# Attention's products as 64x64 tiles in one keys-values section, with its steps named one by one

## The chip, the cores and the metric

The kernel runs on one core of a Trainium2 chip. The metric is the device time of one execution in microseconds (us), the median of several runs.

## The reference

Linear attention over 8 batches, 8 heads, 576 positions and 64 columns per head, followed by a gated feed-forward block that mixes positions. In numpy, cut to what is computed:

```python
kv  = einsum('bhsd,bhse->bhde', k, v)            # keys-values, 64x64 per head
out = einsum('bhsd,bhde->bhse', q, kv)
out = out / sqrt(mean(out*out, -1) + 1e-6) * g_norm
x   = out.transpose(0, 2, 1, 3).reshape(B, S, H * D)      # 8 x 576 x 512
h   = maximum(x @ w_in, 0);  u, v = h[..., :512], h[..., 512:]
v_n = (v - mean(v)) / sqrt(var(v) + 1e-6)
v_s = einsum('ts,bsd->btd', w_spatial, v_n) + b_spatial
y   = (u * v_s) @ w_out                          # 8 x 576 x 512
```

Inputs and outputs are float32.

## The kernel before

Heads go in pairs: four pairs per batch, each 128 columns wide (two heads of 64). The 576 positions are four chunks of 128 and a tail of 64. Feed-forward products are split into a high and a low part and done as three matmuls each in the faster format; attention's own products are plain f32, and each of those shows as two matmul records in the trace.

Per batch the work on TensorE (PE) has these stages, named by the PSUM tiles that they write:
- `psh`: the v half of `x @ w_in`, 4 chunks of 12 products with 512 columns (`hv`), in every second batch also the tails of two batches (`hv_tail`);
- `psua`, `psub`, `psuc`: the u half, 14 steps of 6 products with 288 columns (`u_steps`);
- `psa`, `psb`, `psc`: the mixing over positions and the gate, 14 steps of 6 or 8 products with 288 columns (`sp_steps`, stage p);
- `pso` on `WO`: the output products, 12 with 512 columns per chunk (`out_unit`).

Between them stand the steps of attention for the next batch, its *target batch*:
- keys-values (`pskv`, `att_four`): per pair 10 products, 128 positions by 64 columns by 64 columns, the tail padded with zeros to 128 rows; the results are copied into the diagonal blocks of `KVB` by VectorE (DVE) and ScalarE (ACT);
- queries of pairs 0 and 1 (`pso` on `KVB`, `att_two`): 32 products on 64x64 tiles into two banks, one per half of the rows; then the four pairs' tail queries (`pst`), 64 by 128 columns;
- queries of pairs 2 and 3 (`att_qa`): four products each of 128x128, on a `KVB` block whose off-diagonal quarters are zero;
- a norm per pair (`two_norm`, `norm_a`, `norm_b`), a transpose (`pstr`, `att_t`; `pstt` for the tail) and a split into `XH` and `XL` (`split_x`: ACT for the high part, DVE for the low one).

All of these use three PSUM banks in one pool (`ps_att`, bufs=3); the feed-forward products use four others.

At a batch's start `x_sums` makes eight additions of `XH` and `XL` on DVE and splits four of the sums into `T` and `UX`. `UX` and `WO` share one place in SBUF: `to_u` loads `UX` after the last output product, `to_out` loads `WO` again after the last u product, both from the POOL queue. Keys and values of pairs 2 and 3 are loaded into the place of `U` (`KVU`) once the gates have read it. Loads of keys, values and queries and stores of the output share the queue of SyncE (SP), which issues in order.

What sets the order: text strings hold one token per step. `PLAN` is the opening (to about 77 us). Behind it `FIRST` (batch 1), `EVEN` and `ODD` name v, u, p and o for the next step of each stage, `k` for `att_four` of the next batch, and `s` for the next step of a queue of attention steps, which `att_steps` fills in a fixed order. `SEVEN` and `GATED` hold the order within the u stage and stage p. From this the framework's scheduler builds one static queue per engine: it takes instructions by priority and dependency, and may place an instruction earlier or later than the text has it. Products of attention that are chained (`issue_after`, `high_priority`) follow each other as one run where nothing keeps them.

Of the kernel before, what the change touches and what calls it, by code (L numbers as in the profile page):

```python
# [8 lines left out]
F32 = mybir.dt.float32  # L9
# [34 lines left out]

SEVEN = """

p10 p11 p50 p21 p61 p60 p70 p51 p71 p31 p30 p20 p41 p40
"""
GATED = """

p10 p60 p11 p50 p70 p20 p21 p40 p61 p51 p30 p71 p41 p31
"""
FIRST = """

p p p s p p p p s p s s s p p p p s p p w s o s s o o o w o s s l
# [18 lines left out]
def body(ctx: ExitStack, tc, qT, kvm, kvt, g2, w_in, wsT, bsp, w_out, out):  # L74
# [94 lines left out]
    def tail_queries():  # L169
        return QS.rearrange("q j t -> q (j t)").rearrange("q (p t) -> q p t", t=TAIL)  # L170

    def att_four(b, st):
        banks = [b == 2 and i == 0 or ps_att.tile([P, 512], F32, name="pskv", tag="att") for i in range(2)]
        first = []

        def matmul(*args, **kw):
            if not first:
                first.append(nc.tensor.matmul(*args, **kw).ins)
                return
            with tc.high_priority(), tc.issue_after(first[0]):  # L180
                first[0] = nc.tensor.matmul(*args, **kw).ins  # L181

        for i, ps in enumerate(banks):
            if b == 2 and i == 0:
                continue
            both = ps[:, 0:2 * P].rearrange("p (j e) -> p j e", e=P)
            for j in range(2):
                kv, kt, _ = keys.pop((b, 2 * i + j))
                for c in range(NC + 1):
                    of = kv[:, :, c] if c < NC else kt  # L190
                    for h in (0, D):
                        matmul(both[h:h + D, j, h:h + D], of[:, 0, h:h + D], of[:, 1, h:h + D],
                               start=c == 0, stop=c == NC)
            own = slice(2 * i, 2 * i + 2)
            nc.vector.tensor_copy(KVB[0:D, own, 0:D], both[0:D, :, 0:D])
            nc.scalar.copy(KVB[D:P, own, D:P], both[D:P, :, D:P])
        for p in range(NP):
            st[p] = KVB[:, p]
        att_two(b, st, matmul)
        st["tail"] = ps_tail.tile([P, 512], F32, name="pst", tag="tail")[:, 0:2 * P]  # L200
        for p in range(NP):
# [5 lines left out]
    def att_two(b, st, matmul):  # L207

        qts = [queries.pop((b, i)) for i in range(2)]
        st["two"] = [ps_att.tile([P, 512], F32, name="pso", tag="att") for _ in range(2)]  # L210
        for c in range(NC):
            for j in range(2):
                for half in (0, D):
                    for h in (0, D):
                        at, t = (j * NC + c) * D, c * P + half
                        matmul(st["two"][h // D][half:half + D, at:at + D], qts[j][h:h + D, t:t + D],
                               st[j][h:h + D, h:h + D], start=True, stop=True)

    def two_norm(st, h):
# [3 lines left out]
        nc.scalar.activation(x, heads(ps), AF.Square)  # L223
        nc.vector.tensor_reduce(ss, x, axis=AX.X, op=ALU.add)
        r = rsqrt(ss, 8, P, 1.0 / D, "h")
        nc.vector.tensor_tensor(x, heads(ps), r.unsqueeze(2).broadcast_to([P, 8, D]), op=ALU.mult)
        st[h] = X2[h]
# [95 lines left out]
    def att_q(b, p, st):  # L323
        att_qa(b, p, st, b > 1 and True)
        att_qb(b, p, st)

    def tail_a(b, st, accumulate=False, soon=False):
        st["xt"] = norm_a(st["tail"], P, accumulate, soon)

# [36 lines left out]
    def att_steps(b):  # L366

        st = states.setdefault(b, {})

        def t2():  # L370
            att_t(b, 2, st)
            tail_a(b, st)
            tail_b(b, st)

        def tail():
            tail_a(b, st)
            tail_b(b, st)

        K = [lambda p=p: att_k(b, (p, p + 1), st) for p in (0, 2)]
        Q = [lambda p=p: att_q(b, p, st) for p in range(NP)]  # L380
        T = [lambda p=p: att_t(b, p, st) for p in range(NP)]
        end = lambda: att_tail(b, st)
        if b > 1:
            N = [lambda h=h: two_norm(st, h) for h in range(2)]
            late = [T[0], T[1], Q[2], Q[3], T[2], T[3]]
            if b % 2 == 0:
                return [*[K[0], lambda: att_four(b, st)] * (b == 2), *N, *late[:4], t2, T[3], end], []
            return [*N, lambda: (tail_a(b, st, soon=True), tail_b(b, st)), end], [*late, move_tail]
        if b % 2 == 0:
            return [*K[:1], Q[0], Q[1], T[0], *K[1:], Q[2], T[1], Q[3], t2, T[3], end], []  # L390
        return K + [tail, end], [Q[0], Q[1], T[0], Q[2], T[1], Q[3], T[2], T[3], move_tail]


    def three(ps, pairs):

# [620 lines left out]

    ahead(len(todo))

    def first():

        for c in (0, 2, 1, 3):
            hv(1, c)
            step()
        for d in range(4):
            if d == 2:
                enqueue(2)
            for j in range(2):
                u_unit(1, d, j)
                step()
            if d < 2:  # L1030
                make_out(2 + d)
                split_out(2 + d)
                if loads:
                    loads.pop(0)()

    def batch(b):

        if b > 1:
            to_u()
            x_sums()  # L1040
        v, u, p, o = [0, 2, 1, 3], u_steps(), sp_steps(b), [0, 1] + [NC] * (b % 2) + [2, 3]
        n_w = 0
        for token in (FIRST if b == 1 else ODD if b % 2 else EVEN).split():
            if token == "v":
                hv(b, v.pop(0))
            elif token == "u":
                u.pop(0)()
                if not u:
                    to_out()
                    if b % 2 == 0:  # L1050
                        enqueue(b + 1, 1)
            elif token == "p":
                p.pop(0)()
            elif token == "k":
                if b + 1 < NB:
                    att_four(b + 1, states.setdefault(b + 1, {}))
                enqueue(b + 1)
            elif token == "l":
                if b + 2 < NB:
                    for p in (2, 3):  # L1060
                        att_load(b + 2, p, "e")
            elif token == "o":
                out_unit(b, o.pop(0))
            elif token == "s":
                step()
            elif token == "y":
                step(len(queue))
                hv_tail()
            elif token == "w":
                w_sums(n_w)  # L1070
                n_w += 1
        if b % 2 == 0:
            step(len(queue))

    first()
    for c in range(NC):
        out_unit(0, c)
        step()
    for b in range(1, NB):
        batch(b)  # L1080


_OUTS = [((B, S, DM), "float32")]
# [41 lines left out]
```

## Time and profile before

| | us |
|---|---|
| three runs | 493.8, 493.88, 494.62 |
| median | 493.88 |
| profiled execution | 492.32 |
| its span (first to last instruction) | 490.5 |
| PE busy | 479.6 (98%) |
| DVE busy | 383.0 (78%) |
| ACT busy | 276.1 (56%) |
| share of PE in the chain that ended last | 85% |

Busy time of PE counts overlapping matmuls as modelled by the profiler; what a product costs in a run of products is the distance from its start to the next start. Views used below: the page's head, the list of what each engine waited for, the timeline of one engine in a short stretch, busy times by stretch, the chain that ended last, and groups of instructions by line.

### The profile page before, as it was taken

Reading aid. Unit: us, or ns where it says so; the run is one execution under the profiler, and the core shown is the slowest. Engines: PE = TensorE matmul, PEld = TensorE weight load, DVE = VectorE, ACT = ScalarE, POOL = GpSimd, SP = SyncE. Lnnn points to the kernel's source line nnn. Section 1 sums busy time; section 2 is a strip of 40 time slices with the busy share of each in tenths; the row PEclk is TensorE's granted clock in tenths of the full one; section 3 lists DMA queues with packets and bytes.
Section 4 is the critical chain, followed back from the end, with each engine's and each line's share of the span. In section 5 each row is a group of like instructions: output and inputs, shape, how many; then the busy total and the mean of one; then the engine's idle time right before and its main releaser. Section 6 shows DMA issues by size and latency. Waiting matters only on the chain.

```text
span 490.5 us, 10188 instructions
## 1 busy us (share of the span) xinstructions
PE 479.6 (98%) x3804; PEld 432.9 (88%) x3804; DVE 383.0 (78%) x1029; ACT 276.1 (56%) x818; POOL 35.7 (7%) x71
## 2 busy tenths in 40 slices
PE   6999989999999999999999999999999999999996
PEld 6879988999988899889987899879998889989995
DVE  2889888885977797777895798977887779877770
ACT  3899745867426782378324684257633678246322
POOL 5001100000111010010000000010000101010000
PEclk9999999999999999999999999999999999999999
DMA  8999333643368036461635426362424702333403
GB/s 263 366 303 322 95 103 99 195 165 117 111 244 249 12 91 244 158 209 45 214 126 166 151 76 229 116 194 97 119 99 145 219 1 69 137 103 113 143 31 107
DMA packets 30357, 74.13 MB, mean 151 GB/s; under 512 B 6786, under 2 KB 9858, under 8 KB 28772
## 3 DMA queue, kind: packets, MB, share of 16 engines
q1 hardware_dynamic: 24628, 47.25, 29.9%
q0 software_dynamic: 5456, 25.87, 15.9%
q8 instruction: 30, 0.49, 0.4%
q10 hardware_dynamic: 224, 0.36, 0.2%
q14 instruction: 19, 0.16, 0.1%
HBM read 58.09 MB, written 13.11 MB: 145 GB/s over the span
## 4 chain that ended last, share of the span: by engine, by line
PE 85%; DVE 3%; ACT 2%; DMA 2%; issue 0%; DVEq 0%
PE pso L398 21%; PE psh L431 16%; PE psb L638 7%; PE psub L638 6%; PE psa L638 6%; PE psc L638 5%; PE psuc L638 4%; PE psua L638 4%; PE pskv L181 3%; PE psu L398 3%; PE pstr L341 2%; PE pso L313 2%; DMA stage<-w_out 2%; PE psh L398 2%; PE pso L181 1%; PE psc L644 1%
## 5 line engine op out<-in xcount | busy, mean ns | idle before, releaser
L398 PE MATMUL pso<-WO,G 128*128 128x512 f32 x384 | 95.6, 395 | 0.0
L398 PEld LDWEIGHTS pso<-WO,G 128*128 128x128 f32 x384 | 70.6, 188 | 15.1 <-issue 0.9
L434 ACT CAST G<-SUMg 128x288 fp32r<-128x288 f32 (+1 forms) x56 | 22.2, 405 | 62.0 <-DVE SUMg L660 62.0
L740 ACT COPY o<-pso 128x512 f32<-128x512 f32 x35 | 19.7, 588 | 53.1 <-PE pso L398 44.2
L435 DVE TENSOR_TENSOR VL<-v,VH 128x512 fp32r<-128x512 f32 (+1 forms) x60 | 36.4, 615 | 10.9 <-ACT VH L434 10.6
L431 PE MATMUL psh<-WVH,XH 128*128 128x512 f32 x112 | 43.8, 391 | 0.0
L431 PE MATMUL psh<-WVH,XL 128*128 128x512 f32 x112 | 43.7, 391 | 0.0
L431 PE MATMUL psh<-WVL,XH 128*128 128x512 f32 x112 | 43.6, 390 | 0.0
L434 ACT CAST VH<-v 128x512 fp32r<-128x512 f32 (+1 forms) x60 | 32.8, 563 | 11.9 <-DVE v L463 11.3
L418 ACT ACTIVATE v<-v,mv,rv 128x512 f32<-128x512 f32 x28 | 22.8, 813 | 7.7 <-DVE mv L417 6.1
L410 DVE BATCH_NORM_STATS2 s<-v 128x6 f32<-128x512 f32 x32 | 22.1, 691 | 5.4 <-ACT v L404 4.7
L638 PE MATMUL psb<-WSH,VH 128*128 128x288 f32 x84 | 25.1, 300 | 0.0
L431 PEld LDWEIGHTS psh<-WVH,XL 128*128 128x128 f32 x112 | 21.0, 188 | 4.6
L435 DVE TENSOR_TENSOR G<-SUMg,G 128x288 fp32r<-128x288 f32 (+1 forms) x56 | 23.4, 420 | 2.2
L431 PEld LDWEIGHTS psh<-WVL,XH 128*128 128x128 f32 x112 | 21.0, 188 | 4.4
L431 PEld LDWEIGHTS psh<-WVH,XH 128*128 128x128 f32 x112 | 21.0, 188 | 4.3
L638 PE MATMUL psb<-WSL,VH 128*128 128x288 f32 x84 | 24.7, 295 | 0.0
L638 PE MATMUL psb<-WSH,VL 128*128 128x288 f32 x84 | 24.1, 294 | 0.0
L404 ACT ACTIVATE v<-psh 128x512 f32<-128x512 f32 x32 | 19.1, 598 | 6.3 <-PE psh L431 5.8
L334 ACT ACTIVATE XH<-pstr,gcol 128x512 fp32r<-128x512 f32 x28 | 18.7, 688 | 5.3 <-PE pstr L341 5.3
L638 PE MATMUL psa<-WSH,VH 128*128 128x288 f32 x72 | 21.5, 298 | 0.0
L638 PE MATMUL psa<-WSH,VL 128*128 128x288 f32 x72 | 21.2, 295 | 0.0
(281 smaller groups left out, 1410.9 us busy)
## 6 DMA issues: line engine op xcount, KB each, us to landing
WO<-spare_o POOLq DMA_DIRECT2D x12, 1024.0 KB, 7.0
KV<-kvm SPq DMA_DIRECT2D x19, 512.0 KB, 6.2
UX<-spare_u POOLq DMA_DIRECT2D x18, 512.0 KB, 6.1
out<-o SPq DMA_DIRECT2D x32, 256.0 KB, 2.2
qt<-qT SPq DMA_DIRECT2D x28, 256.0 KB, 4.1
U<-kvm SPq DMA_DIRECT2D x12, 512.0 KB, 4.1
stage<-w_in SPq DMA_DIRECT2D x8, 512.0 KB, 7.4
stage<-w_out SPq DMA_DIRECT2D x4, 512.0 KB, 6.2
```

The costliest lines, as they stand in the source:

```text
L181: first[0] = nc.tensor.matmul(*args, **kw).ins
L313: nc.tensor.matmul(ps[:, c * P:(c + 1) * P], qt[:, c * P:(c + 1) * P], st[p], start=True, stop=True)
L334: nc.scalar.activation(hi, ps, AF.Copy, scale=gcol)
L398: nc.tensor.matmul(ps, lt, rh, start=i == 0, stop=i == n - 1)
L404: nc.scalar.activation(v, ps, AF.Relu)
L410: nc.vector.bn_stats(s6, v)
L418: nc.scalar.activation(v, v, AF.Identity, bias=m, scale=r)
L431: nc.tensor.matmul(ps, lt, rh, start=k == 0 and i == 0, stop=k == NP - 1 and i == 2)
L434: nc.scalar.copy(hi, x)
L435: nc.vector.tensor_tensor(lo, x, f32(hi), op=ALU.subtract)
L638: nc.tensor.matmul(ps, lt, rh, start=start and i == 0, stop=stop and i == len(pairs) - 1, skip_group_check=True)
L740: nc.scalar.copy(o, ps)
```

## The change

From target batch 2 on:
- the queries of pairs 2 and 3 are done as those of 0 and 1 (`att_two` with `first=2`): 32 products on 64x64 tiles into two banks, normed by `two_norm`, which for them takes 8 small squares per half with a running sum;
- the tail queries are 64x64 tiles on two banks (`att_q4`), normed by `two_tail`;
- from batch 3 on the keys-values of all four pairs are one section (`kv_four`) in the order 2, 3, 0, 1, on two banks. The key tails of two pairs lie in one tile of 128 rows, loaded by one DMA, and are 64-row products at the section's end. Batch 2 keeps its two halves (`att_k`, `kv_two`);
- the queue of steps is gone. Each step has its own token: k keys-values, q first queries and tail queries, L second queries, N M n m norms, 0 to 3 transposes, x and e the tail, j the moved tail columns, Q a part of w_out. All five strings are new, `START` replaces `first()`, and `run` replaces `batch`.

The diff, cut to its core:

```diff
 GATED = """
-p10 p60 p11 p50 p70 p20 p21 p40 p61 p51 p30 p71 p41 p31
+p11 p10 p60 p50 p70 p61 p20 p21 p40 p51 p30 p71 p41 p31
 EVEN = """
-k s v v u y v u v s s u u u s u u s u s u s u s u u u s u p p s p p p s p p s s p s s s p p s p p p
-p o o l o o s
+k q u v x v e v u y u v u u u u N u u M u u u u u 1 p p 0 p p p p L p p m p p n p p p 2 p o l o o 3
+j o
 ODD = """
-v v k v v s u u u u u u u u u u s u u u u p s s p p s p s p p p p s s p p p p s p s p o l o s s o o
+k v u v u v q v u M u u u u u u u u u u p N 1 0 p L n m p p p p p p p p 2 p x e 3 p p p o l o o o
 o
@@ att_load
-            (nc.scalar if (b, p) == (0, 0) else nc.sync).dma_start(kt[0:TAIL], kvt[b, p])
+            if b < 3:
+                (nc.scalar if (b, p) == (0, 0) else nc.sync).dma_start(kt[0:TAIL], kvt[b, p])
+            else:
+                kt = KT[2 + p // 2]
+                if p % 2 == 0:
+                    nc.sync.dma_start(kt, kvt[b, p:p + 2].rearrange("p t x e -> (p t) x e"))
@@
-    def att_four(b, st):
...
+    def att_q4(b, st, matmul):
         att_two(b, st, matmul)
-        st["tail"] = ps_tail.tile([P, 512], F32, name="pst", tag="tail")[:, 0:2 * P]
-        for p in range(NP):
-            r, c = slice(p % 2 * TAIL, (p % 2 + 1) * TAIL), slice(p // 2 * P, (p // 2 + 1) * P)
-            matmul(st["tail"][r, c], tail_queries()[:, p], st[p], start=True, stop=True)
+        st["tail"] = [ps_tail.tile([P, 512], F32, name="pst", tag="tail"),
+                      ps_att.tile([P, 512], F32, name="pst", tag="att")]
+        for j in range(2):
+            for i in range(2):
+                p, r, c = 2 * j + i, slice(i * TAIL, (i + 1) * TAIL), slice(j * D, (j + 1) * D)
+                for h in (0, D):
+                    matmul(st["tail"][h // D][r, c], tail_queries()[h:h + D, p],
+                           KVB[h:h + D, p, h:h + D], start=True, stop=True)
         issue()
         issue()
+    def kv_four(b, matmul):
+
+        banks = [ps_att.tile([P, 512], F32, name="pskv", tag="att") for _ in range(2)]
+        both = [ps[:, 0:2 * P].rearrange("p (j e) -> p j e", e=P) for ps in banks]
+        of = {p: keys.pop((b, p)) for p in range(NP)}
+        order = (2, 3, 0, 1)
+        for n, p in enumerate(order):
+            kv, to = of[p][0], both[p % 2]
+            for c in range(NC):
+                for h in (0, D):
+                    matmul(to[h:h + D, p // 2, h:h + D], kv[:, 0, c, h:h + D], kv[:, 1, c, h:h + D],
+                           start=n < 2 and c == 0, stop=False, skip_group_check=True)
+        for j in (1, 0):
+            kt = of[2 * j][1]
+            for i in range(2):
+                r = slice(i * TAIL, (i + 1) * TAIL)
+                for h in (0, D):
+                    matmul(both[i][h:h + D, j, h:h + D], kt[r, 0, h:h + D], kt[r, 1, h:h + D],
+                           start=False, stop=True, skip_group_check=True)
+        for i in range(2):
+            nc.vector.tensor_copy(KVB[0:D, i:NP:2, 0:D], both[i][0:D, :, 0:D])
+            nc.scalar.copy(KVB[D:P, i:NP:2, D:P], both[i][D:P, :, D:P])
@@ att_two(b, st, matmul, first=0)
-            for j in range(2):
+            for j in (1, 0):
                 for half in (0, D):
-                    for h in (0, D):
+                    for h in (D, 0):
@@ two_norm(st, h, first=0)
+        if first:
+            for k in range(8):
+                nc.scalar.activation(x[:, k], ps[:, k * D:(k + 1) * D], AF.Square,
+                                     accum_out=ss[:, k:k + 1])
@@ two_tail(st, soon)
+        for h in range(2):
+            nc.scalar.activation(own[h], ps[h], AF.Square)
+        nc.vector.tensor_reduce(ss, heads(x), axis=AX.X, op=ALU.add)
+        r = rsqrt(ss, 4, P, 1.0 / D, "h").rearrange("p (j g) -> p j g", g=2)
+        for h in range(2):
+            nc.vector.tensor_tensor(own[h], ps[h], r[:, :, h].unsqueeze(2).broadcast_to([P, 2, D]),
+                                    op=ALU.mult)
```

What that makes of the queues, at three places. In these rows a count behind x is of instructions; a row names line, operation, output and inputs, and the output's shape.

PE at the end of batch 2's output stage (target batch 4), before: two keys-values runs of one pair (`pskv`) stand between output products, the second with the queries behind it.

```order
L398 MATMUL pso_2612<-WO,G 128x512
L181 MATMUL pskv<-U 64x64 x8
L181 MATMUL pskv<-KT_106 64x64 x2
L398 MATMUL pso_2632<-WO,G 128x512 x7
L398 MATMUL pso_2648<-WO,G 128x512
L181 MATMUL pskv<-U 64x64 x8
L181 MATMUL pskv<-KT_107 64x64 x2
L181 MATMUL pso<-KVB,qt 64x64 x32
L181 MATMUL pst<-KVB,QS 64x128 x4
L398 MATMUL pso_2648<-WO,G 128x512 x6
L431 MATMUL psh<-WVH,XH 128x512
```

The other two pairs' run (10 products each, on `KV_102` and `KV_103`) stood in the middle of stage p. The same place after:

```order
L463 MATMUL pso_2681<-WO,G 128x512 x3
L187 MATMUL pskv<-U 64x64
L190 MATMUL pskv<-U 64x64 x15
L190 MATMUL pskv<-KV_102 64x64 x8
L190 MATMUL pskv<-KV_103 64x64 x8
L190 MATMUL pskv<-KT_107 64x64 x4
L190 MATMUL pskv<-KT_106 64x64 x4
L496 MATMUL psh<-WVH,XH 128x512
```

One run of 40 products stands behind all output products; the queries and tail queries have moved on into the psh stage, 24 psh and 12 psua products later.

PE in batch 2's u stage, before: the two query products of 128x128 (x4 each) stand apart.

```order
L431 MATMUL psh<-WVH,XL 128x512
L313 MATMUL pso<-KVB,qt 128x128 x4
L638 MATMUL psuc<-T,UX 128x288 x6
...
L638 MATMUL psub<-T,WUL 128x288
L313 MATMUL pso<-KVB,qt 128x128 x4
L638 MATMUL psub<-T,UX 128x288 x6
```

After, the second queries are one run there, 6 psub products behind the last psh; the 8 transposes of pairs 0 and 1 stand 42 products ahead (24 psh, 6 psuc, 6 psua and these 6 psub):

```order
L496 MATMUL psh<-WVH,XL 128x512
L703 MATMUL psub<-T,WUH 128x288 x2
L703 MATMUL psub<-T,WUL 128x288
L703 MATMUL psub<-T,WUH 128x288 x2
L703 MATMUL psub<-T,WUL 128x288
L187 MATMUL pso<-KVB,qt 64x64
L190 MATMUL pso<-KVB,qt 64x64 x31
L703 MATMUL psub<-T,UX 128x288 x6
```

The 128x128 query products are gone, and 32 products of 64x64 stand in one place.

DVE at the turn from batch 1 to batch 2, after: the copies into `KVB` stand behind the last of the eight additions of `x_sums` and ahead of the four splits into `T`.

```order
L607 TENSOR_TENSOR SUMu_111<-SUMu_111,SUMp_110 128x576
L608 TENSOR_TENSOR SUMg<-SUMg,SUMu_111 128x576
L240 COPY KVB<-pskv 64x2x64 x2
L500 TENSOR_TENSOR T<-SUMu_111,T 128x576
L500 TENSOR_TENSOR T<-SUMp_110,T 128x576
```

Before, one copy stood in stage p and one behind the additions; now both stand behind them.

## Rows read from the trace of the kernel before

**Rows 1.** The page's head: span, TensorE's busy time, its granted clock

```profile
span 490.5 us, 10188 instructions
...
PE 479.6 (98%) x3804; PEld 432.9 (88%) x3804; DVE 383.0 (78%) x1029; ACT 276.1 (56%) x818; POOL 35.7 (7%) x71
...
PEclk9999999999999999999999999999999999999999
```

**Rows 2.** What PE waited for: us in total, times, longest

```profile
PE pskv L236 <- DMA KV<-kvm: 2.9, 3, 1.5
PE pstr L341 <- DVE x L305: 1.3, 1, 1.3
PE pso L313 <- ACT KVB L254: 1.1, 2, 0.8
```

**Rows 3.** Busy by stretch: stretch, length, PE, PEld, DVE, ACT, POOL, clock, DMA

```profile
268.00:326.50 58.50, 58.48 (x481) 52.57 (x480) 47.13 (x127) 32.98 (x100) 3.78 (x7) 1.00 0.44 147
326.50:384.50 58.00, 58.00 (x480) 52.38 (x479) 46.92 (x129) 30.59 (x96) 2.67 (x5) 1.00 0.41 134
```

**Rows 4.** PE's timeline, stage p: start, length, line, tiles, shapes, count

```profile
300.06 0.27 PE L181 MATMUL pskv<-KV 128*64 128x64 f32 x1
...
301.37 0.40 PE L638 MATMUL psc<-WSH,VH 128*128 128x288 f32 x1
```

**Rows 5.** PE's timeline in the output stage that follows

```profile
319.05 0.62 PE L398 MATMUL pso<-WO,G 128*128 128x512 f32 x2
319.61 0.69 PE L181 MATMUL pskv<-U 128*64 128x64 f32 x16
...
320.34 2.11 PE L398 MATMUL pso<-WO,G 128*128 128x512 f32 x8
322.38 0.69 PE L181 MATMUL pskv<-U 128*64 128x64 f32 x16
...
323.11 1.16 PE L181 MATMUL pso<-KVB,qt 64*64 64x64 f32 x64
324.20 0.66 PE L181 MATMUL pst<-KVB,QS 128*64 128x128 f32 x8
324.79 0.51 PE L398 MATMUL pso<-WO,G 128*128 128x512 f32 x1
```

**Rows 6.** The chain that ended last: start, length, what

```profile
285.40 0.89 PE pso L313 x8
...
289.48 0.89 PE pso L313 x8
...
346.38 2.41 PE psub L638 x18
...
428.66 8.94 PE pso L398 x39
```

**Rows 7.** PE's timeline: two first output products

```profile
197.48 0.63 PE L398 MATMUL pso<-WO,G 128*128 128x512 f32 x2
...
310.64 0.39 PE L398 MATMUL pso<-WO,G 128*128 128x512 f32 x1
```

**Rows 8.** DVE's timeline: the last addition

```profile
204.73 0.76 DVE L543 TENSOR_TENSOR SUMg<-SUMg,SUMu 128x576 f32<-128x576 f32 x1
```

**Rows 9.** Groups by line: shapes, count, busy us, mean ns, idle before

```profile
L335 DVE SCALAR_TENSOR_TENSOR XL<-pstr,gcol,XH 128x512 fp32r<-128x512 f32 x28 | 20.5, 739 | 0.2 <-ACT XH L334 0.2
...
L334 ACT ACTIVATE XH<-pstr,gcol 128x512 fp32r<-128x512 f32 x28 | 18.7, 688 | 5.3 <-PE pstr L341 5.3
...
L195 DVE COPY KVB<-pskv 64x128 f32<-64x128 f32 x11 | 3.1, 280 | 8.6 <-PE pskv L181 8.5
...
L196 ACT COPY KVB<-pskv 64x128 f32<-64x128 f32 x11 | 2.9, 260 | 6.3 <-DVE KVB L195 6.2
```

**Rows 10.** POOL's timeline: the weights' reload issued

```profile
297.84 1.11 POOL L979 DMA_DIRECT2D WO<-spare_o  x2 [6.09 <-PE psuc L638]
```

**Rows 11.** Tile WO: its loads and stores, issue to landing

```profile
DMA to landing us min/median/max: 2.0/5.4/10.0
```

More of the change, by code (lines that the diff above doesn't have):

```diff
@@ L170, in tail_queries, with chain @@
         return QS.rearrange("q j t -> q (j t)").rearrange("q (p t) -> q p t", t=TAIL)
-    def att_four(b, st):
-        banks = [b == 2 and i == 0 or ps_att.tile([P, 512], F32, name="pskv", tag="att") for i in range(2)]
-        first = []
+    def chain(behind=None):
+        last = []
         def matmul(*args, **kw):
-            if not first:
-                first.append(nc.tensor.matmul(*args, **kw).ins)
+            if not last:
+                with tc.issue_after(behind) if behind else ExitStack():
+                    last.append(nc.tensor.matmul(*args, **kw).ins)
@@ L197, in att_four @@
[L197 to L203 removed]
+            with tc.high_priority(), tc.issue_after(last[0]):
+                last[0] = nc.tensor.matmul(*args, **kw).ins
@@ L204, in att_four, with kv_two @@
         issue()
         issue()
-    def att_two(b, st, matmul):
-        qts = [queries.pop((b, i)) for i in range(2)]
+    def kv_two(b, matmul):
+        ps = ps_att.tile([P, 512], F32, name="pskv", tag="att")
+        both = ps[:, 0:2 * P].rearrange("p (j e) -> p j e", e=P)
+        for j in range(2):
+            kv, kt, _ = keys.pop((b, 2 + j))
+            for c in range(NC + 1):
+                of = kv[:, :, c] if c < NC else kt
+                for h in (0, D):
+                    matmul(both[h:h + D, j, h:h + D], of[:, 0, h:h + D], of[:, 1, h:h + D],
+                           start=c == 0, stop=c == NC)
+        nc.vector.tensor_copy(KVB[0:D, 2:4, 0:D], both[0:D, :, 0:D])
+        nc.scalar.copy(KVB[D:P, 2:4, D:P], both[D:P, :, D:P])
@@ L219, in two_norm @@
-    def two_norm(st, h):
+                               KVB[h:h + D, first + j, h:h + D], start=True, stop=True)
+    def two_norm(st, h, first=0):
         ps = st["two"][h]
@@ L325, in att_q, with two_tail @@
         att_qb(b, p, st)
+    def two_tail(st, soon):
+        if soon:
+            x = work.tile([P, 512], F32, name="xt", tag="stg", bufs=2)[:, 0:2 * P]
+        else:
+            x = X2[0][:, 0:2 * P]
+        own = [x.rearrange("p (j g e) -> p j g e", g=2, e=D)[:, :, h] for h in range(2)]
+        ps = [b[:, 0:2 * D].rearrange("p (j e) -> p j e", e=D) for b in st["tail"]]
+        ss = small.tile([P, 8], F32, name="ss", tag="ss")[:, 0:4]
+        for h in range(2):
[5 more added lines that the diff above has]
+                                    op=ALU.mult)
+        st["xt"] = x
     def tail_a(b, st, accumulate=False, soon=False):
@@ L1017, in body, with run, outs, hvs @@
     ahead(len(todo))
[L1019 to L1032, printed above, removed]
+    def run(b, tokens, v, u, p, o):
+        n_w, made = 0, iter((2, 3))
+        for x in tokens.split():
+            if x in "kqLNMnm0123xej":
+                if b + 1 < NB:
+                    att_token(x, b + 1)
+                continue
+            row.clear()
+            if x in "vupo":
+                {"v": v, "u": u, "p": p, "o": o}[x].pop(0)()
+                if x == "u" and not u and b > 1:
+                    to_out()
+            elif x == "l":
+                if b + 2 < NB:
+                    for i in (2, 3):
+                        att_load(b + 2, i, "e")
+            elif x == "y":
+                hv_tail()
+            elif x == "w":
+                w_sums(n_w)
+                n_w += 1
+            elif x == "Q":
+                k = next(made)
+                make_out(k)
+                split_out(k)
                 if loads:
                     loads.pop(0)()
-    def batch(b):
+    def outs(b):
+        return [lambda c=c: out_unit(b, c) for c in [0, 1] + [NC] * (b % 2) + [2, 3]]
+    def hvs(b):
+        return [lambda c=c: hv(b, c) for c in (0, 2, 1, 3)]
+    run(1, START, hvs(1), [lambda d=d, j=j: u_unit(1, d, j) for d in range(4) for j in range(2)], [], outs(0))
+    for b in range(1, NB):
         if b > 1:
@@ L1040, in batch @@
             x_sums()
[L1041 to L1080, printed above, removed]
+        run(b, FIRST if b == 1 else ODD if b % 2 else EVEN, hvs(b) * (b > 1), u_steps() * (b > 1), sp_steps(b), outs(b))
 _OUTS = [((B, S, DM), "float32")]
```

88 lines of the change are left out of this document (45 added, 43 removed).

## The prediction

> **What bounds the kernel now.** I began with the page's head: TensorE (PE) is busy for 479.6 of 490.5 us, at the full clock in all 40 slices [rows 1]. Busy time is modelled, so I went on to the wait list of PE: its longest entries, 2.9 and 1.3 us on L236 and L341, belong to the opening, and the same list asked for from 77.5 us on is empty [rows 2]. In the middle of the kernel one batch takes about 58 us, in which PE is busy throughout and VectorE (DVE) for 47 us, ScalarE (ACT) for 31 to 33 us [rows 3]. So behind the opening the time is the sum of what stands in PE's queue. Work taken out of that queue shortens the kernel by as much, as long as nothing makes PE wait; work moved on other engines is worth nothing by itself.
>
> So the prediction has two halves: how much shorter PE's queue becomes, and whether the new order makes it wait.
>
> **PE's queue, before.** In the timeline I read starts, not durations, because neighbouring matmuls overlap; the gap from one start to the next is what an instruction costs. An f32 product is two records (the program has 32 query products where the trace has x64). For a target batch from 3 on, attention's products stand in five places:
> - keys-values of two pairs in stage p, 40 records: 300.06 to 301.37, 1.31 us [rows 4];
> - one pair between output products, 20 records: 319.61 to 320.34, 0.73 us [rows 5];
> - the other pair, then the queries of two pairs as 64x64 tiles, then the tail queries: 322.38 to 324.79, of which 0.73, 1.09 (64 records) and 0.59 us [rows 5];
> - two query products of 128x128 (pairs 2 and 3), 0.89 us each [rows 6].
>
> Going from 128x128 work to narrow tiles and back costs too: the eight output products between the two sections take 2.04 us [rows 5] where 39 of them back to back take 8.94, or 0.229 each [rows 6], so eight should take 1.83. One leaving and one entering cost 0.21 us; three sections, 0.63. Sum before: 1.31 + 0.73 + 2.41 + 1.78 + 0.63 = **6.86 us per batch**.
>
> **PE's queue, after.** Rates from the same rows: 20 more keys-values records cost 1.31 - 0.73 = 0.58 us, 0.029 each, and what is left of 0.73, 0.15, is the fixed part of a run in one form. A 64x64 record then costs (1.09 - 0.15) / 64 = 0.0147. The new order has, per batch,
> - one section with 32 keys-values products and 8 of the tails as 64x64 tiles: 64 x 0.029 + 0.15 = 2.01, and 16 x 0.0147 + 0.15 = 0.39;
> - the first queries and the tail queries in one form: 80 x 0.0147 + 0.15 = 1.33;
> - the other two pairs' queries: 1.09, as the same 64 records cost today;
> - three times 0.21 = 0.63.
>
> Sum 5.45: **1.41 us less per batch**, five times (batches 3 to 7), 7.05. Most of it is the two 128x128 query products (1.78 against 1.09 + 0.21, 0.5), the tail queries (0.35) and the fixed parts of runs that are joined. Batch 2 gains less: its keys-values stay as they are, the tail queries save 0.59 - 0.24 = 0.35, and the second queries are torn: the program has one product, two output products, then the other 31, which adds 0.21 + 0.15, so 1.66 against 1.78. Together 0.47. **PE's queue is 7.5 us shorter.**
>
> The form that the trace doesn't have is the tail of the keys (64 rows by 64 columns on k and v). Its nearest row is the 64x64 query tile, which I take; at the dearer rate of the column form it would cost 16 x 0.0143 = 0.23 more per batch, 1.1 in all; below it there is no row, since no product in the trace comes closer than these.
>
> The Trainium skill has a rule against such small tiles: TensorE: Matmul & The Clock Gate, section "Wait — 56ns, not 53.3ns?", says that start-to-start never drops below about 25 ns however small the product is. By it 64 records would take 1.6 us, and the second queries with their 0.21 would gain nothing on 1.78. The trace says otherwise: 64 records in 1.09 us is 17 ns each [rows 5].
>
> **The other engines.** The second queries' norm keeps its 16 small squares on ACT and its one reduction chain per half; the tail's norm becomes two half-width squares and products, some 0.2 us more on ACT and DVE, which have 25 and 11 us to spare per batch [rows 3]. The four copies into KVB stay four. Two of four key-tail loads fall away. The last batch has no attention in it, before or after, and ends with the same 51 output products. The opening's order changes in a few places of ACT, DVE and PE; nothing is added there, so I count nothing, with 1 us either way.
>
> **Where the new order could make PE wait.** Three places.
>
> *First queries behind the KVB copies.* All four pairs now finish together, and DVE has the eight additions of x_sums ahead of the copies. Before, the last product of stage p ends at 197.48 [rows 7], the last addition at 204.73 + 0.76 = 205.49 [rows 8]: 8.0 us. After, 43 output products (43 x 0.229 = 9.8) and the section (2.4) come first, so DVE is free over 4 us before it has to copy. The copies take 0.28 on DVE and 0.26 on ACT each [rows 9]; the queries stand 24 psh and 12 psua products (7.1 us) behind in even target batches and 12 + 4 long and 6 short ones (4.5 us) in odd ones. No wait.
>
> *Second queries behind PSUM banks.* The pool has three banks (`bufs=3`), and two hold the transposes of pairs 0 and 1 just ahead. Those banks come free when ACT (0.69 each) and DVE (0.74 each) have split them [rows 9]. In even target batches 18 products (2.4 us) stand between. In odd ones the split must wait until the last psh run has read that pair of XH, and 0.8 us of psub stand between: if the splits begin when pair 0 and pair 1 have been read (9 and 6 products, 2.1 and 1.4 us before the run's end), they are done about 0.25 us behind it and hide; if they begin at its end they take 0.69 x 2 + 0.74 = 2.1 and PE waits 1.3.
>
> *The weights' reload.* WO is loaded again after the last u product and needed by the first output product. Before, POOL issues both halves at 297.84 [rows 10] and the product starts at 310.64 [rows 7], with landings of up to 10.0 us [rows 11]. After, 81 products at 0.134 [rows 6] and 8 transposes (1.8, at the price of the 128x128 query products) stand between, 12.6 us; issue (about 1.1 for the second half) and the worst landing make 11.1, so 1.5 us are left.
>
> I take no new wait, since two of the three have room and the third begins early in PE's order.
>
> **The rivals.**
> 1. *The bank wait is half real*: 0.65 us at each of six second queries, +3.9 us: **490.3**. For it: DVE is at 81% and its queue in that stretch also holds layer-norm steps. Against: the splits can start before the run ends. Chance 0.16.
> 2. *WO arrives late* (the slower end): if its second half lands more than 11.5 us after its issue, each of six batches' first output products waits. From 1.25 us late per batch on the gain is gone; at 1.9 late it is 7.5 - 11.4 = +3.9, **497.8**. For it: the cover shrinks from 12.8 us behind the issue to about 12.0, and loads of queries share the queues. Against: worst landing 10.0. Chance 0.06.
> 3. *Small tiles are not that fast in the new places*, because tiles in another order block each other: 64x64 records at the column form's 0.029 cost 0.0143 x (16 + 16 + 64) = 1.37 more per batch, for six batches +8.2: **494.6**. Against: the same form runs at 17 ns [rows 5]. Chance 0.02. A floor per start, as the Trainium skill has it in the section named above, would act in this way.
> 4. *The change hardly does anything*, a mixture of torn sections and small waits that eats 6.5 to 8.5 us: **493.9**, chance 0.04.
>
> **How the numbers follow.** The profiled execution is 492.3 us, span 490.5; the runs' median is 493.88, 1.6 above it. The gain is absolute, so I take it off the median: 493.88 - 7.5 = **486.4**. Chance 0.72 within 2 us of that. The range for 8 in 10 goes from 484.5 (the sum, 1 us of the opening, and 0.8 for the spread of the runs) to 491.0 (rival 1 whole, and the dearer tails). 0.2% is about what a measurement of this kernel can tell from no change, so faster is below 492.9: the forecast and rival 1, 0.88; same, rival 4 and half of rival 3, 0.05; slower, rival 2 and the other half, 0.07.
>
> **What would show it.** In the profile after: PE's span share unchanged near 98% and no entries in its wait list behind the opening; keys-values of all pairs in one run of 80 records, about 2.4 us; second queries 1.09 us at 17 ns per record; a batch at about 56.6 us instead of 58. The step on banks is wrong if PE's start of the second queries lies more than 0.1 us behind the psub before it in odd target batches; the step on WO if the first output product waits for a DMA. The forecast falls as a whole if six such waits of over 1 us stand in PE's list.

## The result and the profile after

The changed kernel takes 488.46 us (median of 6 runs, 487.56 to 490.51) beside 494.24 us of the kernel before on the same chip: a ratio of 0.9885, interval 0.9862 to 0.9908, that is 5.8 us less (4.6 to 6.8). The forecast was 7.5 us less, 486.4. The profiled execution took 489.41 us, its span 487.6.

The page of the profile after, its head (share of the span and instructions of each engine, busy tenths and granted clock in 40 slices), to be read against [rows 1]:

```profile
span 487.6 us, 10839 instructions
PE 474.9 (97%) x4140; PEld 427.1 (88%) x4140; DVE 381.4 (78%) x1035; ACT 274.8 (56%) x824; POOL 35.8 (7%) x71
PE   6999989999999999999999999999999999999996
PEclk9999989999999999999999999999999999999999
```

TensorE is still busy nearly throughout, and it has 4.7 us less work. But one slice in the opening is below the full clock, and the wait list, which was empty behind the opening before [rows 2], has three entries now. The wait list of TensorE from 79.3 us to the end (waiting tile, what released it, us in total, times, longest):

```profile
PE psh L463 <- ACT XH L392: 0.7, 1, 0.7
PE psc L703 <- DVE SUMg L723: 0.3, 1, 0.3
PE psub L703 <- DVE U L666: 0.2, 1, 0.2
```

The pieces that the prediction priced are there as priced. TensorE's timeline around the keys-values section and the first queries of one batch (start, modelled duration, line, tile, shape, records):

```profile
205.65 0.27 PE L187 MATMUL pskv<-U 128*64 128x64 f32 x1
...
207.66 0.46 PE L190 MATMUL pskv<-KT 64*64 64x64 f32 x16
208.05 0.50 PE L496 MATMUL psh<-WVH,XH 128*128 128x512 f32 x1
...
215.31 0.27 PE L187 MATMUL pso<-KVB,qt 64*64 64x64 f32 x1
...
215.42 1.05 PE L190 MATMUL pso<-KVB,qt 64*64 64x64 f32 x59
216.29 0.41 PE L190 MATMUL pst<-KVB,QS 64*64 64x64 f32 x16
216.63 0.50 PE L496 MATMUL psh<-WVH,XH 128*128 128x512 f32 x1
...
228.96 0.69 PE L703 MATMUL psub<-T,UX 128*128 128x288 f32 x4
229.59 0.27 PE L187 MATMUL pso<-KVB,qt 64*64 64x64 f32 x1
...
230.68 0.40 PE L703 MATMUL psuc<-XH,UX 128*128 128x288 f32 x1
```

Start to start: the 64 long records of the keys-values 2.01 us (forecast 2.01), the 16 of the tails 0.39 (0.39), first and tail queries 1.32 (1.33), second queries 1.09 (1.09). The second queries begin 0.63 us after the first of four psub products (4 x 0.133 = 0.53, and 0.09 for the change of form): no wait for a bank.

**An account of the whole.** Behind the opening, from the first psh run on, every kernel of this study runs the same 2103 large products (128x288 and 128x512). At their undisturbed rates, 0.1326 and 0.2285 us from start to start, they take 355.9 us. What is left of TensorE's time I split by the record at which it falls: the start-to-start times of all narrow records with the entering and the wait in front of each run of them ("narrow"), and what a large product with another large one behind it takes above its rate ("gaps"; what the first large product behind a narrow run takes more, the leaving of the form, is among it). Worked out from all records of each profile:

| kernel | median us | narrow | gaps | both |
|---|---|---|---|---|
| before | 494.2 | 47.5 | 5.2 | 52.7 |
| before_again | 494.2 | 48.4 | 5.3 | 53.8 |
| changed | 488.5 | 41.5 | 6.6 | 48.1 |
| after_again | 488.4 | 40.9 | 6.9 | 47.8 |
| cover | 490.0 | 42.3 | 7.0 | 49.3 |
| nolow | 487.1 | 41.6 | 4.9 | 46.5 |
| pool | 487.6 | 40.8 | 6.1 | 46.9 |
| whole | 496.3 | 44.9 | 10.2 | 55.0 |
| old_seven | 495.2 | 43.6 | 11.2 | 54.8 |
| pool_y2 | 494.2 | 41.3 | 11.3 | 52.7 |
| m0_pool | 499.5 | 45.1 | 10.9 | 56.0 |
| m0 | 497.6 | 45.6 | 12.6 | 58.2 |
| y2 | 500.5 | 43.3 | 15.7 | 58.9 |
| old_places | 516.2 | 59.5 | 15.5 | 74.9 |

Median less the last column is 439 to 442 in all but m0_pool (443.5), and 440.4 to 441.5 for the kernel before and the changed one: the medians are explained by this one column. It comes from one execution each, and two profiles of one kernel differ by 1.0 us (before) and 0.3 (changed), so less than that says nothing.

In the first pair of profiles narrow records give 6.0 us less and gaps 1.4 more. Two single waits at the end of narrow runs are new: 0.9 us behind the transpositions that begin at 277.0, where the gate tail's product waits for ScalarE's split, and 0.3 behind the second queries at 286.8. The first in TensorE's timeline:

```profile
277.02 1.03 PE L399 MATMUL pstr<-ident,xx 128*128 128x128 f32 x8
278.72 0.50 PE L463 MATMUL psh<-WVH,XH 128*128 128x512 f32 x1 [0.66 <-ACT XH L392]
```

Of the gaps, 4.1 us in the kernel before (43 narrow runs) and 3.5 in the changed one (36 runs) are the leaving of a narrow form; all other gaps grew from 1.2 to 3.1 us. So the forms gave 6.0 + 1.2 + 0.6 = **7.8 us**, against 7.5 in the forecast, and new waits took 1.2 + 1.9 = **3.1 us** back. The second pair (before_again and after_again, below) gives 7.6 and 2.7 us in the same way; there the kernel before had 1.1 us of waits of its own, 0.9 of them at one tail query. The last column fell by 4.7 us in the first pair and by 6.0 in the second, the medians by 5.8 and 5.9.

### The profile page after: what moved, and what is told of

Its sections match the earlier page's. It is cut to its first block, busy times and chain, and to the rows that moved or that the text cites. A ratio compares the mean times of both kernels' runs of the same rounds, so it can differ in the third digit from the quotient of the medians.

```text
span 487.6 us, 10839 instructions
## 1 busy us (share of the span) xinstructions
PE 474.9 (97%) x4140; PEld 427.1 (88%) x4140; DVE 381.4 (78%) x1035; ACT 274.8 (56%) x824; POOL 35.8 (7%) x71
## 4 chain that ended last, share of the span: by engine, by line
PE 75%; DVE 11%; ACT 7%; DMA 4%; issue 2%; SPq 0%; ACTq 0%; DVEq 0%
PE pso L463 19%; PE psh L496 15%; PE psb L703 6%; PE psa L703 5%; PE psc L703 4%; PE psub L703 4%; PE psua L703 3%; PE psuc L703 3%; PE psu L463 3%; PE pstr L399 2%; PE pskv L190 2%; DMA stage<-w_out 2%; PE pso L190 2%; DVE TA L546 1%; DMA out<-o 1%
## 5 line engine op out<-in xcount | busy, mean ns | idle before, releaser
L463 PE MATMUL pso<-WO,G 128*128 128x512 f32 x384 | 94.3, 394 | 0.0
L500 DVE TENSOR_TENSOR T<-SUMu,T 128x576 fp32r<-128x576 f32 x12 | 9.0, 754 | 16.8 <-ACT T L499 11.5
```

The costliest lines, as they stand in the source:

```text
L463: nc.tensor.matmul(ps, lt, rh, start=i == 0, stop=i == n - 1)
L500: nc.vector.tensor_tensor(lo, x, f32(hi), op=ALU.subtract)
```

## Experiments

Line numbers are each kernel's own. Three groups of four ran on one chip each, beside the kernel before: cover, whole, nolow and before_again; after_again, m0, pool and m0_pool; the rest.

**cover**: TensorE's idle stretch in the opening filled.

```diff
-s T12 s s B11 M0 W T11 B13 M1
+s T12 s s B11 M0 W T11 f9 B13 M1
...
+        for _ in range(n):
+            ins = nc.tensor.matmul(ps[:, 0:P], KVB[:, 1], KVB[:, 1], start=True, stop=True).ins
```

> The changed kernel with nine 128x128 products more, of values that nobody reads, between the first tail products of the opening and the transposes of pair 3, where TensorE stood idle from 65.6 to 67.8 us; all other instructions stand in the order of the changed kernel. Nine such products take 2.0 us (18 records at 0.111), so they fit the idle time. Theory (the granted clock fell to half from about 69 to 72 us because TensorE had stood idle for 2 us, and that is the 1.64 us by which the opening grew): the clock stays at 1.00 in every slice, the keys-values run behind it takes 1.3 instead of 1.9 us, the first run of psh starts near 77.7 instead of 79.3, and the time falls by 1.6 us, to about 487 us. Rival (the clock falls for what comes behind the idle time, narrow tiles that wait for a DMA): it falls again at 69 us and the time stays at 488.5, or grows by up to 0.3.

The changed kernel's first profile, windows of the opening (us, length, busy time and instructions of each engine, granted clock, DMA share and GB/s):

```profile
66.00:67.00 1.00, 0.00 (x0) 0.00 (x0) 0.91 (x4) 0.00 (x0) 0.00 (x1) 1.00 0.96 215
...
69.00:70.00 1.00, 1.00 (x26) 1.00 (x22) 0.77 (x2) 0.12 (x1) 0.00 (x0) 0.50 0.00 0
70.00:71.00 1.00, 1.00 (x9) 0.88 (x6) 0.41 (x2) 0.26 (x1) 0.00 (x0) 0.50 0.96 262
71.00:72.00 1.00, 1.00 (x5) 0.82 (x4) 1.00 (x4) 0.00 (x0) 0.00 (x0) 0.50 0.95 344
```

Half the granted clock, 1.2 GHz, for some 3 us, after TensorE had waited 2.05 us for VectorE. In cover TensorE's timeline there reads:

```profile
68.94 2.17 PE L719 MATMUL psw<-KVB 128*128 128x128 f32 x18
71.16 0.63 PE L401 MATMUL pstr<-ident,x 128*128 128x128 f32 x4
71.71 0.69 PE L277 MATMUL pskv<-KV 128*64 128x64 f32 x16
```

The clock stayed full there, the keys-values took 1.3 us, and the stretch from the transposes of pair 1 to the first psh run took 13.9 us instead of 15.0. But the time did not fall: 489.96 us, ratio 0.9921 (0.9886 to 0.9955). The next runs suggest a reason: the fall is not in every execution. The theory's "1.00 in every slice" failed too: in this profile the clock was half from 14.1 to 17.5 us instead.

**before_again** and **after_again**: both kernels unchanged.

> The kernel before, unchanged, to see the granted clock of its timed executions. Its profiled execution took 492.3 us at a mean clock of 1.00, its timed ones 493.8 to 495.3. Theory (its opening has an idle stretch of TensorE of 1.5 us, in some executions longer, and then its clock falls too): executions near 494 show mean clocks of 0.993 to 0.998, and those near 492 show 1.00. Rival (the difference has nothing to do with the clock): 1.00 in all of them.

> The changed kernel, unchanged, beside its variants on the same chip. In its first profile the stretch of the opening from the transposes of pair 1 (64.28 us) to the first run of psh (79.30) took 15.0 us where the kernel before took 12.3, of which 1.64 us at half the granted clock; behind it the same large products (355.9 us) ran with 6.6 us of gaps and 41.5 us of narrow products. Theory (the loss in the opening comes from VectorE's order there and is in every execution; the fall of the clock comes on top in some): the stretch takes 13.2 to 15.2 us again, the rest 404 to 405 us, the median 488 to 490. Rival (the first profile was an unlucky one): 12.3 us and 487.

The kernel before took 494.22 us (492.0 to 495.7), with mean clocks of 0.993 to 1.00 that do not go with the times: 495.7 at 1.00, 492.0 at 0.997. So the theory failed; of the rival, that the times don't go with the clock held, but the clock is not 1.00 in all executions. The changed kernel took 488.35 us (ratio 0.9891, 0.9858 to 0.9924); its stretch of the opening took 12.9 us at full clock, shorter than I expected, where the kernel before takes 12.3 in both profiles. In nolow and pool, with the same order there, TensorE waited 2.0 us; in nolow the clock fell (15.2 us), in pool it did not (13.9). Earlier in the opening, beginning between 10.9 and 14.1 us, the clock was half for some 3 us in seven of the fourteen profiles (before_again, cover, nolow, whole, m0_pool, y2, old_places) and full in the other seven. The stretch has grown by 0.6 to 2.9 us, then, but other parts of the opening vary by as much from one execution to the next, and the medians show nothing of it.

**nolow** and **pool**: VectorE's gate-tail subtractions left out, and made on GpSimd.

The edit of pool, where `eng` is `nc.gpsimd` in the stages of even batches; nolow leaves the line out there:

```diff
-                nc.vector.tensor_tensor(TA[i][other, cols], x[own], f32(hi), op=ALU.subtract)
+                eng.tensor_tensor(TA[i][other, cols], x[own], f32(hi), op=ALU.subtract)
```

> The changed kernel without the twelve subtractions on VectorE that make the low halves of the gate tail's values (TA) in the stages of even batches, four in each, 2.3 us of VectorE per stage; that part of the computation is left out. TensorE's and ScalarE's orders are unchanged. Theory (in the even stages TensorE waits for PSUM banks that VectorE empties late, since these subtractions stand ahead of the additions into U): the excess of 0.86 us per stage around psub and psa (174 to 190 us in the first of them) goes to below 0.2, three times, so 2 to 2.5 us faster than the changed kernel, about 486.2. Rival (the banks are freed late by ScalarE, or the excess is TensorE's own, from changes of form): less than 0.5 us faster.

> The changed kernel with the twelve subtractions of the gate tail's low halves in even stages made on GpSimd instead of VectorE; TensorE's order hardly changes. Leaving them out took 1.7 us of gaps from between the large products. Theory (VectorE's lateness is all that matters there, and GpSimd has 93% of its time free): gaps between large products 5.0 us as without them instead of 6.6, 1.5 us faster than the changed kernel. Rival 1 (GpSimd is so slow at them that the tail products of the spatial stage, or the loads that GpSimd issues behind them, come late): new waits of the first products with TB or WO, slower by 1 us or more. Rival 2 (both engines slow each other): VectorE's operations beside them take longer than their usual 0.45 and 0.69 us, and the gain is under 0.5 us.

The changed kernel at the end of stage u, TensorE and VectorE, lines of other engines left out:

```profile
176.41 1.40 DVE L546 TENSOR_TENSOR TA<-v,TA 64x512 fp32r<-64x512 f32 x2
...
177.26 0.95 PE L703 MATMUL psub<-T,UX 128*128 128x288 f32 x6
177.84 0.46 DVE L681 TENSOR_TENSOR U<-psub,U 128x288 f32<-128x288 f32 x1
178.22 0.45 DVE L686 TENSOR_TENSOR U<-psuc,U 128x288 f32<-128x288 f32 x1
178.36 0.40 PE L703 MATMUL psa<-WSH,VH 128*128 128x288 f32 x1
```

Six products from 177.26 end their queue time at 178.06; psa begins at 178.36, when its bank has been emptied by an addition that stood behind two subtractions of 0.7 us. The same place in nolow:

```profile
179.21 0.46 DVE L682 TENSOR_TENSOR U<-psub,U 128x288 f32<-128x288 f32 x1 [0.30 <-PE psub L704]
...
179.81 0.96 PE L704 MATMUL psub<-T,UX 128*128 128x288 f32 x6
180.00 0.46 DVE L687 TENSOR_TENSOR U<-psuc,U 128x288 f32<-128x288 f32 x1 [0.34 <-PE psuc L704]
180.60 0.29 PE L704 MATMUL psa<-WSH,VH 128*128 128x288 f32 x1
```

Now VectorE waits for TensorE, and psa follows after 0.79 us without a gap. Gaps fall from 6.6 or 6.9 to 4.9 us, with TensorE's and ScalarE's orders unchanged; without the leaving of narrow forms that is from 3.1 or 3.4 to 1.4, beside 1.2 in the kernel before. So most of the new gaps between large products are VectorE's lateness, as the theory had it. The time alone would not show it: 487.08 us is 1.3 to 1.4 less than the changed kernel, where 2 to 2.5 were forecast, and its interval (0.9820 to 0.9899) overlaps that of after_again. On GpSimd the long subtractions take 1.29 us each instead of 0.69, and the reload of WO behind them still waits for TensorE's last product of stage u (psuc), not for them. The group in the list of lines (busy us, mean ns, idle before), and the reload in GpSimd's timeline:

```profile
L546 POOL TENSOR_TENSOR TA<-v,TA 64x512 fp32r<-64x512 f32 x6 | 7.7, 1289 | 68.2 <-ACT TA L545 68.0
```

```profile
182.00 1.11 POOL L1044 DMA_DIRECT2D WO<-spare_o  x2 [0.95 <-PE psuc L703]
```

VectorE's additions beside them keep their 0.45 us. Narrow and gaps together fell by 0.9 to 1.2 us, gaps alone to 6.1 rather than 5.0. The time, 487.56 us beside 488.35 on the same chip (ratios 0.9870, 0.9841 to 0.9899, and 0.9891), is too close to call it better.

**whole**: the second queries as 128x128 products again.

```diff
-                att_two(b, st, row["matmul"], 2)
+                whole_two(b, st, row["matmul"])
...
+                matmul(ps[:, c * P:(c + 1) * P], qt[:, c * P:(c + 1) * P], KVB[:, p],
+                       start=True, stop=True)
```

> The changed kernel with one part undone: the second queries (pairs 2 and 3) as eight 128x128 products instead of 64 of 64x64 (they are split over two records each), at the same place of the program; their norms have the same 16 squares and two products. Theory (the sum of the prediction): 1.78 us instead of 1.09 + 0.21 in five batches, and 1.78 instead of 1.66 in batch 2: 2.5 us slower, 491.0. Rival 1 (small tiles cost a floor of some 25 ns each, or the narrow form costs as much at its two ends as it saves): the same within 0.5 us. Rival 2 (the norms of half heads make the new waits of the stages u and p): faster, by up to 1 us.

496.28 us, 7.9 more than the changed kernel, neither theory's number nor either rival's. The products themselves are as priced: 1.70 us from their first start (230.63) to the next product (232.33), against 1.09 + 0.09.

```profile
230.63 0.38 PE L187 MATMUL pso<-KVB,qt 128*128 128x128 f32 x2
230.85 1.73 PE L190 MATMUL pso<-KVB,qt 128*128 128x128 f32 x14
232.33 0.38 PE L723 MATMUL psub<-UX,WUH 128*128 128x288 f32 x1
```

Narrow records grew by 3.4 to 4.0 us, of which 2.5 were forecast. The rest, 3.3 to 3.6 us, is gaps: with the other tiles the scheduler put the products of stages u and p into another order, too. So I looked at what order alone does.

**m0** and **m0_pool**: a step of the opening moved; no work changed.

```diff
-s T12 s s B11 M0 W T11 B13 M1
+s T12 s s B11 W T11 M0 B13 M1
```

> The changed kernel with one step of the opening (the first mixing of the spatial weights, whose first two additions stood on VectorE ahead of the gate tail's subtractions) put behind the transposes of pair 1 in the program; pair 3's product with its norm then comes 0.85 us earlier on VectorE. Behind the opening several engines' orders shift too. Theory (VectorE's order in the opening makes TensorE idle there for 2.2 us and lets the clock fall): the stretch from the transposes of pair 1 to the first psh run takes 12.3 to 13.0 us instead of 15.0, with the clock at 1.00; by that alone the time falls by 2 to 2.7 us. Rival (the stretch is bound by a DMA: the keys' load, or the copy of the tail's halves): within 0.5 us of 15.0. What the shifted orders behind cost is not known: they may give 3 us of waits back, and then the time is the same as the changed kernel's.

> Both changes, the mixing step moved in the opening and the subtractions on GpSimd. Theory (two places that don't touch each other): the two gains add, 3.5 to 4 us faster than the changed kernel, about 485. Rival (the order behind the opening, which shifts with every edit, costs as much): no better than the better of the two alone.

The stretch of the opening took 12.9 us, and 12.3 in m0_pool, as the theory said; but the unmoved kernel took 12.9 in after_again too, so m0 shows nothing of the move. And the time was 497.55 us (ratio 1.006, 1.0034 to 1.0086) and 499.45: the scheduler's order shifted in all later batches, and narrow and gaps together rose to 58.2 and 56.0 us, where m0_pool was forecast to be 3.5 to 4 us faster than the changed kernel. TensorE's wait list of m0 from 83 us on:

```profile
PE pstt L407 <- DVE xt L381: 2.8, 1, 2.8
PE psb L703 <- DVE SUMu L773: 1.3, 1, 1.3
PE pso L463 <- ACT U L591: 0.9, 1, 0.9
```

The first of these waits ends at 167.96 us, and from 170.1 to 173.5 the granted clock was half; the large products in it took 1.6 us above their rate, which stands among m0's gaps.

**y2** and **pool_y2**: the gate tail's product two steps later in even stages.

```diff
-k q u v x v e v u y u v u u u u N
+k q u v x v e v u u v y u u u u N
```

> The changed kernel with one step of the even stages moved: the product of the gate tail stands one product of stage u and one of the values later, since TensorE waited 0.5 to 0.9 us there in one or two of the three stages for ScalarE's split of the tail (277.0 us in the first profile). Theory (a local wait, gone with the distance): narrow products 40.3 instead of 40.9 to 41.5, gaps as before, 0.5 to 1 us faster. Rival (the order that the scheduler works out behind the edit shifts and costs as much as the mixing step did): 3 to 10 us slower, in gaps between large products.

> The same move, together with the gate tail's subtractions on GpSimd, which by themselves took 0.9 us off the time behind the opening. Theory: 1.5 to 2 us faster than the changed kernel, 486.5 to 487. Rival (the shifted order decides): 3 us or more slower, like the move alone.

500.46 us and 494.18, 12.0 and 5.7 us above the changed kernel: the rival held both times, in y2 beyond the 10 us that it gave. The longest waits of y2, from 83 us on, are VectorE's again. With the subtractions on GpSimd it is 6.3 us less, but that edit shifted TensorE's order once more, so how much of it is VectorE's relief stays open:

```profile
PE psub L703 <- DVE U L675: 2.7, 5, 0.7
PE psuc L703 <- DVE U L676: 1.5, 3, 0.5
PE pstr L399 <- DVE xx L267: 1.4, 1, 1.4
```

**old_seven** and **old_places**: the order undone, first of the seven products alone, then of everything.

```diff
 SEVEN = """
-p11 p10 p50 p60 p70 p61 p21 p51 p71 p30 p40 p20 p41 p31
+p10 p11 p50 p21 p61 p60 p70 p51 p71 p31 p30 p20 p41 p40
...
 ODD = """
-k v u v u v q u v u M u u u u u u u u u u p N 1 0 p L n m p p p p p p p p 2 p x e 3 p p p o l o o o
-o
+v v k q v v N u u u u u u u u u u M u u u u p 0 1 p p L p n m p p p p 2 x 3 p p p p e p p o l o o o o
```

> The changed kernel with one part undone: the seven products of the stages u and p in their old order; attention's tiles and steps as in the changed kernel. The prediction counted this part of the change at nothing. Theory (it is worth what VectorE's lateness makes of it, which no step of the sum held): gaps between large products grow or shrink by 1 to 6 us from 6.6 to 6.9 us, narrow products stay at 41; no sign is forecast. Rival (VectorE is early enough for either order): 488.4 within 0.5 us.

> The changed kernel's tiles at the places of the kernel before: the same 64x64 products, one keys-values section, norms of half heads; but the seven products of the stages u and p in their old order, and every attention step where the old queue put it (the first queries right behind the keys-values, the second ones behind the transposes of pairs 0 and 1 in stage p). Theory (the gain is the shorter queue of narrow products; the order only has to hide the copies and banks): narrow products take about 41 us behind the opening as in the changed kernel, and TensorE waits for the copies into KVB and for VectorE some 0.5 to 1 us more per batch, 3 to 6 us in all: 491 to 494. Rival 1 (the order is what gains, the tiles hardly matter): all of it is lost, 494 or more, with narrow products above 46 us. Rival 2 (the order matters for nothing): 488.4, as the changed kernel.

old_seven takes 495.21 us (ratio 1.0017, 0.9995 to 1.0038): this one part of the change, which the prediction counted at nothing, undoes the whole gain when it is missing (with the shifts that the scheduler makes behind it, as in y2), with 4.3 to 4.6 us more of gaps and 2.1 to 2.7 more in the narrow records. old_places takes 516.21 us, 22 us above the kernel before: far outside the theory, and within the first rival's numbers (494 or more, narrow above 46) but not by its cause, for about 14 us of its 59.5 narrow are five waits, and the runs of records at full clock are as fast as in the changed kernel. TensorE's wait list from 82 us on:

```profile
PE pstt L405 <- DVE xt L379: 9.7, 2, 8.8
PE pso L185 <- DVE XL L391: 2.6, 2, 2.2
PE psub L701 <- DVE U L664: 1.3, 3, 0.9
```

The second line is the bank wait that the prediction had as its first rival: the second queries of an odd stage wait 2.2 us for the split of the transposes. The first is a transposition of the tail's values (one, 8.8 us at 400 to 409) that stands in TensorE's queue while VectorE is still busy with other work ahead of their norm. The granted clock was half from 403.7 to 414.0 us, from within this wait on, and a transposition there took 213 ns from start to start instead of 109.

## Why the prediction was right, and where it was not

**The queue of narrow products: right.** 7.8 and 7.6 us from forms in the two pairs of profiles against 7.5; each run of records has its forecast length to 0.02 us. The key tails took the cheaper of the two rates. In the rows 59 records of 64x64 take 0.87 us (215.42 to 216.29), 14.7 ns each. The Trainium skill (TensorE: Matmul & The Clock Gate, "Wait — 56ns, not 53.3ns?") gives a floor of about 25 ns from start to start, and the trace does not agree with it. Undoing the second queries priced them at 1.70 against 1.09 + 0.09 us, 0.5 per batch as forecast.

**A batch at 56.6 us: not quite.** Two batches from one keys-values section to the next (205.65 to 320.68) took 115.0 us, 57.5 each, and 57.2 in after_again, beside 58.2 in the kernel before (206.08 to 322.38): the waits are in them.

**The three waits that I looked for: right.** No first output product waited for WO, the first queries did not wait for KVB, and the second queries not for their banks. For WO the sum was too long, though: it prices eight transposes at 1.8 us, and they took 0.79; in even stages the first output product began 11.2 us behind POOL's first issue, not 12.6, and was in time since no landing took over 8.5. The timelines of POOL and TensorE, and the landings of WO:

```profile
182.26 1.11 POOL L1044 DMA_DIRECT2D WO<-spare_o  x2 [3.03 <-DVE U L681]
...
186.64 1.03 PE L399 MATMUL pstr<-ident,xx 128*128 128x128 f32 x8
187.43 0.38 PE L703 MATMUL psb<-WSH,VH 128*128 128x288 f32 x1
...
193.49 1.30 PE L463 MATMUL pso<-WO,G 128*128 128x512 f32 x5
...
DMA to landing us min/median/max: 2.0/5.2/8.5
```

old_places shows that the bank wait is real and larger than my bound (2.2 against 1.3 us) where the order doesn't avoid it.

**"I take no new wait": wrong, by 3.1 us in the first pair of profiles and 2.7 in the second.** I read 47 of 58 us of VectorE per batch [rows 3] as 11 us to spare and asked only at three places. The failed step is to take a mean share as room: the additions that empty PSUM banks stand in VectorE's queue behind whatever the order puts ahead of them, and 0.3 us of lateness there is 0.3 us of TensorE. nolow showed this for 1.7 to 2 us of it; the wait for ScalarE's split at 277.0, 0.9 us in the first profile and 0.3 in after_again, is of another kind, and what makes it late was not tested. The wait list shows 1.2 us of the 3.1 only; the rest are gaps too short for it, and are seen in start-to-start times alone.

**The opening, "counts nothing, 1 us either way": right for the median, for a reason I did not have.** One stretch of it grew by 0.6 to 2.9 us, with TensorE waiting for VectorE's norm in it; that VectorE's changed order there is the cause was argued, and m0 did not show it. What made the clock fall behind an idle stretch of 2.0 us in two profiles and not in a third (pool) stays open.

**The chance for a slower kernel was argued from the wrong place.** It rested on WO's reload and on half of a rival about slow tiles. Five orders of the same tiles (old_seven, y2, m0, m0_pool, pool_y2) measured from the time of the kernel before to 6 us above it, and old_places 22 us above. That the order written in the change is among the good ones could not be read from the profile of before; the forecast held because it is, and that part of it was luck.

## What to carry to other kernels

Price a queue from start-to-start times of its own rows, and it will hold to a few tenths; then ask for each PSUM bank what stands ahead of the instruction that empties it, because an engine at 80% can still be late at a bank. Where a scheduler works out the order, a gain of 1% in tiles and the order it was measured in are one change: carried to another order it can be lost several times over, so compare several orders, and separate work from waits in each profile before judging a tile.

## What the runs showed of the hardware that I had not expected

64x64 records in the same form followed each other at 14.7 ns, in new places as in the old one. TensorE's granted clock fell to 1.2 GHz for some 3 us in two profiles (the changed kernel's first one from 68.9 us, nolow's from 69.5) after some 2 us of waiting for VectorE, and stayed at 2.4 GHz in pool after as long a wait. It also fell behind single waits in the middle of the kernel: in m0 from 170.1 us, 2.1 us after a wait of 2.8, and in old_places for 10 us from within the wait of 8.8. GpSimd needs 1.29 us for a subtraction of 64x512 that VectorE makes in 0.69, and VectorE's additions beside it were not slower than 0.45 us.
